# Block 0's last sums on VectorE, w_in's sums later on GpSimd, step 7's q and k ahead of a row of w_out

## The chip, the cores and the metric

The kernel runs on one core of a Trainium2 chip. The metric is the device time of one execution in microseconds; the kernel before took 661.88 us (median of three runs, 661.77 to 662.99). A core has five engines that run side by side, each with its own queue in which instructions start in order: TensorE (PE in the profile) multiplies matrices and writes to PSUM, VectorE (DVE) and ScalarE (ACT) do elementwise work, GpSimd (POOL) does elementwise work between SBUF tiles, and SyncE (SP) only starts transfers (DMAs). ACT and POOL start transfers too.

## The reference

Two stages. The first is a recurrent retention over 4 batches, 8 heads and 768 steps with heads of 64; its output, with the heads side by side, is the input x of 3072 tokens by 512. The second is a feed-forward layer with a quick GELU:

```
state = gamma * state + k_t v_t^T          (per batch and head)
y_t   = scale * q_t state
x     = y as 3072 x 512
h     = x @ w_in                           (512 x 2048)
out   = (h * sigmoid(1.702 h)) @ w_out     (2048 x 512)
```

All of it is computed in float32; the weights arrive as 64-bit floats.

## The kernel before

**Tiling.** The retention is done in chunks of 64 steps for two batches at once: 24 chunks, called steps j below. Four steps give the 512 tokens of one block; there are six blocks, m = 0 to 5. Each block goes through an up-projection (w_in, gate) and a down-projection (w_out). While block m is projected, the steps of the block after next are woven in (`step`, `turn`, `decay`), so that TensorE always has work.

**Fewer products.** Most projections are done by a scheme with seven products of half matrices in place of eight. It needs sums and differences of the inputs: of w_in (`sums_w1`, on GpSimd, four instructions for each of four pairs p of row groups), of w_out (`sums_w2`, and its t3 term `sums_w2_t3`, L542, on VectorE), of the gated hidden values g (`sums_g`, L546 to L548, VectorE; `sums_g_late`, L552, GpSimd) and of X (`sums_x`, L530 to L533, GpSimd). Block 0 computes its hidden values with plain products (`up0`) and keeps them where the sums of w_in will later lie: slots 4, 5 and 6 of the weights' tiles W1A and W1B hold its g in slots 0, 1 and 2; slot 3 lies in X and in a small tile g0 whose place is later that of kd. So sums_w1 can write slot 4 only after block 0's g slot 0 has been read for the last time, and so on.

**Stages in time.** 0 to 105 us: eight steps of the retention, the narrowing of the 64-bit weights to float32 (fetch on SP, `abs` on ScalarE, `half` and `rest` on VectorE) and block 0's up-projection, in an order written out by hand. 105 to 154: block 1's up-projection (`seven`). 154 to 204.5: block 0's down-projection. 204.5 to 261.5: block 1's. Then blocks 2 to 5, each some 100 us, with `up` (L562) and `down49` (L666), the last with a second level of seven products.

**Block 0's and 1's down-projection** (`down`, L799) is a list of 28 units, n = 0 to 27, of 1.73 us each: seven products of four units d. Product n // 4 = 2 reads slot 3 of g; after each of its units the three `sums_g` of that pair of rows are made, and the fourth product reads their result. Product 6 (units 24 to 27) reads slot 1 after `sums_g_late`. The third and fourth outputs are stored from GpSimd's queue after product 5 (`then_p7`, `put`), the last after product 6. Between the units the loop at the end of the kernel calls `sums_w2_t3` (block 0, units 8 to 11), `sums_w1` (block 1, units 3, 11, 19 and 27) and `inner_w2` (L612, differences of w_out, stored to W2D in DRAM from SP and GpSimd).

**Blocks 2 to 5** load those differences back: `stream` (L635) fetches for each i = 0 to 6 three pieces of 256 KB into half of a tile `ring`, with one DMA on GpSimd's queue. Piece 1 is read by the third pair of unit (i, 0), the fourth product in TensorE's order there, pieces 0 and 2 by unit (i, 1). The stream for i + 2 is called once the half is free, after unit (i, 1) and after `then`, which makes the output's additions (`put`, GpSimd, L692 to L695) and stores it (L696).

**What sets the order.** TensorE's queue is in the order of the code. On the other engines a scheduler places each instruction when, by its own estimate, its inputs are ready, so an instruction may run far ahead of its place in the code. `tc.keep_in_program_order(i)`, and `pin` as long as `ordered` is set, tie an instruction behind the one that the code issued before it on the same engine. In the first stage all is tied. `decay` (kd, L274) and `aged` (state, L359) of steps 9 and later are not.

**Loads.** Steps 6 and 7 load q and k in 8 DMAs each on SP (L157), then k again as kn and v (L143). `w9b w9a` in the written order are the two fetches (L180) of one row of w_out. From step 8 on, kn has a single buffer, which `decay` frees; `turn` transposes q and k on VectorE (L253) and then loads those two steps ahead.

Of the kernel before, what the change touches and what calls it, by code (L numbers as in the profile page):

```python
# [28 lines left out]
def kernel(  # L29
# [29 lines left out]
    pe, act, dve, pool, sp = nc.tensor, nc.scalar, nc.vector, nc.gpsimd, nc.sync  # L59
# [13 lines left out]
    NP = NFF // 2  # L73
# [19 lines left out]
    W2D = [dram.tile([P, 3, NP // 2, P], F32, name=f"W2D{i}") for i in range(7)]  # L93
    W2 = const.tile([P, 7, NP, EH], F32, name="W2")
# [426 lines left out]
    def sums_w1(p):  # L521
        t, q1 = w1(p)
        w = [t[:, q1:q1 + 2, s] for s in range(7)]
        pool.tensor_add(w[4], w[2], w[3])
        pool.tensor_sub(w[6], w[0], w[2])
        pool.tensor_sub(w[5], w[4], w[0])
        pool.tensor_sub(w[2], w[1], w[5])

    def sums_x():
        tc.keep_in_program_order(pool.tensor_sub(X[:, 4], X[:, 2], X[:, 0]))  # L530
# [8 lines left out]
        dve.tensor_sub(w[1], w[2], w[5])  # L539

    def sums_w2_t3(p):
        dve.tensor_sub(W2[:, 6, p:p + 2, :], W2[:, 5, p:p + 2, :], W2[:, 0, p:p + 2, :])  # L542

    def sums_g(m, p):
        a = [g(m, p, s) for s in range(4)]
# [3 lines left out]

    def sums_g_late(m, p):  # L550
        a = [g(m, p, s) for s in range(2)]
        tc.keep_in_program_order(pool.tensor_sub(a[1], a[1], a[0]))  # L552


    def up(d):
# [76 lines left out]
    def stream(ring, i):  # L632

        c = ring[:, i % 2 * 3:i % 2 * 3 + 3]
        pool.dma_start(c, W2D[i])  # L635
        return c

    def begin_ring():
# [4 lines left out]
    def down49(m, ring, comps):  # L643

        b, t0 = m * CB // NC * 2, m * CB % NC * D
# [37 lines left out]
        def put(th, e, half, y, a):  # L683
            if half == 0:
                kept[th, e] = two.tile([P, 7, P], F32, name="o")
            c = kept[th, e]
            dve.tensor_add(c[:, 4 * half:4 + 3 * half], y, kept[a][half])
            if half == 0:
                return
            last = m == NB - 1  # L690
            eng = dve if last else pool
            eng.tensor_add(c[:, 1:3], c[:, 1:3], c[:, 0:1].to_broadcast([P, 2, P]))  # L692
            eng.tensor_add(c[:, 3], c[:, 3], c[:, 2])
            eng.tensor_add(c[:, 0:5:4], c[:, 2:4], c[:, 4:5].to_broadcast([P, 2, P]))
            eng.tensor_add(c[:, 2:4], c[:, 0:4:3], c[:, 5:7])  # L695
            (act if last else pool).dma_start(rows[th, e], c[:, 1:5].rearrange("p (b f) e -> p b (f e)", b=2))  # L696

        def then(i, half, p0):
            if i == 0:
# [36 lines left out]
        for i in range(7):  # L736
            for half in range(2):
                def unit(i=i, half=half):
                    if half == 0:
                        if i == 0:  # L740
                            pairs[0] = derive(0)
                        x = "x" if i in (0, 2, 3) else "y"
                        if i != 2 and i != 3:
                            for n in range(2):
                                acc[x, n] = ps.tile([P, 4 - n, P], F32, name="pq", tag=x)
                    x = "x" if i in (0, 2, 3) else "y"
                    if i == 6 and half == 1 and m == NB - 1:
                        finish(acc[x, half], pairs[i][half])
                        return
                    products(acc[x, half], pairs[i][half], i not in (2, 3))  # L750
                    then(i, half, acc[x, half])
                    if half == 0 and i < 6:
                        pairs[i + 1] = derive(i + 1)
                    if half == 1:
                        if i + 2 < 7:
                            comps[i + 2] = stream(ring, i + 2)
                        if i in (0, 1, 3):
                            sums_g_outer((0, 1, None, 2)[i])
                todo.append(unit)
        return todo  # L760

    def down(m):

        acc, kept = {}, {}
        b, t0 = m * CB // NC * 2, m * CB % NC * D
# [58 lines left out]
        for n, d in order:  # L824
            key, sa, sb, new, last, then = P_[n]
            def unit(key=key, sa=sa, sb=sb, new=new, last=last, d=d, then=then, n=n):
                part(key, sa, sb, new, last, d, then)
                if n == 2:
                    sums_g(m, 2 * d)
                if n == 4 and d == 3:  # L830
                    for p in range(0, NP, 2):
                        sums_g_late(m, p)
            todo.append(unit)
# [110 lines left out]
    for name in """  # L944
        k0 table q0 warm turn0 w0b rows warm k1 abs0b q1 turned0 step0 v0 w0a half0b mask k2 turn1 causal rest0b
        masked0 decay0 v1 decay1 abs0a half0a step-0 updated0 turned1 q2 step1 rowd whole w2b turn2 w2a x0 k3
        aged1 masked1 turned2 v2 rest0a abs2 q3 step-1 updated1 state1 decay2 aged2 step2 q4 x1 half2 decay3 w3b
        w3a up0.0.0 masked2 turn3 k4 step-2 v3 q5 rest2 k5 gate0.0.0 turned3 updated2 state2 step3 up0.0.2
        masked3 abs3 half3 x2 rest3 turn4 w1b step-3 aged3 gate0.0.2 turned4 state3 w1a w5b updated3 v5 decay4
        abs1 x3 turn5 half1 up0.0.3 turned5 up0.1.2 step4 aged4 w5a rest1 v4 gate0.0.3 decay5 w6a masked4  # L950
        gate0.1.2 abs5 w6b step5-4 half5 rest5 up0.0.1 updated4 abs6 state4 gate0.0.1 w4b
        up0.1.1 half6 aged5 w4a up0.0.5 rest6 masked5 up0.1.5 gate0.1.1 x4 gate0.0.5 abs4 step-5 w8b w8a
        half4 gate0.1.5 state5 updated5 anew q6 up0.1.6 x5 rest4 gate0.1.6 abs8 v6 decay6 aged6 up0.0.6 w7b w7a half8
        turn6 gate0.0.6 up0.1.0 abs7 seven_4.2 seven_6.2 half7 gate0.1.0 w9b w9a up0.1.4 q7 gate0.1.4 step6 masked6 rest7 up0.0.4 v7
        gate0.0.4 seven_52.2 turn7 up0.1.3 gate0.1.3 step7-6 seven_4.0 masked7 updated6 decay7 aged7 abs9 state6 x6 up0.0.7 rest8 seven_w.0 gate0.0.7
        w11a w11b step-7 state7 x7 seven_x half9 w10b w10a up0.1.7 gate0.1.7
        seven2.0 seven2.1 abs11 rest9 seven2.2 seven_v.0 w12a w12b seven2.3 half11 seven2.4 abs10 seven_4.1 seven_w.1
        seven2.5 rest11 seven2.6 w14b w14a seven0.0 seven0.1 half10 seven0.2 abs12 seven0.3 rest10 w13a w13b seven0.4
        seven_v.1 seven0.5 seven_4.3 half12 seven_w.3 seven0.6 seven1.0 abs14 seven1.1 rest12 w15a w15b seven1.2 seven1.3
        half14 seven1.4 abs13 seven_v.3 seven1.5 updated7 rest14 seven1.6 seven3.0 seven3.1 half13 seven3.2 abs15 seven3.3  # L960
        rest13 seven3.4 seven3.5 late_loads half15 rest15 seven3.6 seven_end
    """.split():
        works[name]()
    ordered[0] = False
    INNER = [(0, 19), (0, 22), (0, 26), (1, 2), (1, 12), (1, 15), (1, 18)]
    for m in range(NB):
# [31 lines left out]
        for n, unit in enumerate(down(m) if m < 2 else down49(m, *ring)):  # L998
            unit()
            if m == 0 and n < NP and n % 2:  # L1000
                sums_w2(n - 1)
            if m == 0 and NP <= n < 3 * NP // 2:
                sums_w2_t3(2 * (n - NP))
            if m == 1 and n % 8 == 3:
                sums_w1(n // 4)
            if (m, n) in INNER:
                inner_w2(INNER.index((m, n)))
            if between and (n in (2, 5, 11, 16, 21) if m == 1 else n % 3 == (1 if m else 2)):
# [49 lines left out]
```

## Time and profile before

| what | value |
|---|---|
| median of three runs | 661.88 us |
| the profiled execution | 662.24 us |
| its span, from first to last instruction | 660.5 us |
| TensorE busy | 642.2 us (97%) |
| VectorE busy | 453.9 us (69%) |
| GpSimd busy | 198.8 us (30%) |
| ScalarE busy | 159.0 us (24%) |
| chain of waits: TensorE's share | 89% |
| GpSimd idle ahead of the ring's DMAs (L635) | 227.7 us |
| granted TensorE clock | 0.997 of full speed |

A row of the timeline gives the start, the length, the engine, the line of the kernel, the operation, the tile written and the tiles read, the shapes, the number of instructions merged, and in brackets the idle time of the engine just before with the instruction that ended it. A float32 matmul leaves two records. "SPq" is SP starting a DMA. The list of waits gives for each engine and line whom it waited for, in total, how often, and the longest. The chain of waits is followed back from the last instruction, each step to what released it.

### The profile page before, as it was taken

How to read it: one execution, taken by the hardware profiler on the slowest of the kernel's cores; microseconds unless marked ns; L12 is line 12 of the kernel's file. 1: busy time of each engine (PE TensorE's matmuls, PEld its weight loads, DVE VectorE, ACT ScalarE, POOL GpSimd, SP SyncE). 2: the span in 40 equal slices, each digit the busy share in tenths (PEclk: the TensorE clock that was granted, in tenths of full speed). 3: DMA queues.
4: the chain of work that ended last, by engine and by line, in shares of the span. 5: the costliest groups of instructions: out<-in, count | busy, mean ns of one | idle time of the engine just before them, and what ended most of it. 6: DMA issues, size and time to landing. Idle time of an engine off the chain costs nothing.

```text
span 660.5 us, 15291 instructions
## 1 busy us (share of the span) xinstructions
PE 642.2 (97%) x6390; PEld 580.2 (88%) x6390; DVE 453.9 (69%) x645; ACT 159.0 (24%) x306; POOL 198.8 (30%) x225
## 2 busy tenths in 40 slices
PE   6789999999999999999999999999999999999997
PEld 3778888888788888889999888999888999988997
DVE  3699989999936973556984445995354995254965
ACT  4674233551000000333100233010233110233110
POOL 6400311310379217000536400445600255500000
PEclk9989999999999999999999999999999999999999
DMA  9995549763233556262485832386742252602142
GB/s 176 193 274 173 152 104 241 172 163 60 49 82 135 137 149 153 58 248 96 118 199 134 279 57 97 86 223 135 225 118 97 66 154 104 235 21 96 55 154 96
DMA packets 148149, 91.86 MB, mean 139 GB/s; under 512 B 131600, under 2 KB 134416, under 8 KB 147056
## 3 DMA queue, kind: packets, MB, share of 16 engines
q1 hardware_dynamic: 135856, 45.19, 29.8%
q0 software_dynamic: 9888, 44.46, 20.6%
q10 hardware_dynamic: 2336, 1.25, 0.6%
q8 instruction: 50, 0.82, 0.5%
q14 instruction: 19, 0.16, 0.1%
HBM read 72.89 MB, written 15.47 MB: 134 GB/s over the span
## 4 chain that ended last, share of the span: by engine, by line
PE 89%; DVE 4%; DMA 4%; SPq 1%; issue 1%; ACT 0%; DVEq 0%
PE pq L666 27%; PE px L562 17%; PE pd L799 13%; PE py L562 13%; PE ph L491 7%; PE ph L414 5%; PE pa L289 2%; PE py L312 2%; PE pa L297 2%; PE py L306 2%; DMA W<-in_moe_w_in_dram 1%; DMA W<-in_moe_w_out_dram 1%; DMA q_in<-in_q_dram 1%; PE pt L250 1%; SPq L140 1%
## 5 line engine op out<-in xcount | busy, mean ns | idle before, releaser
L635 POOL DMA_DIRECT2D ring<-W2D x28 | 15.4, 551 | 227.7 <-PE px L562 118.3
L666 PE MATMUL pq<-W,G 128*128 128x128 f32 x672 | 80.2, 276 | 0.0
L666 PEld LDWEIGHTS pq<-W,G 128*128 128x128 f32 x672 | 77.6, 192 | 1.3 <-issue 0.7
L666 PE MATMUL pq<-ring,own 128*128 128x128 f32 x448 | 60.1, 276 | 1.3 <-issue 1.3
L562 PE MATMUL px<-X,W1A 128*128 128x256 f32 x256 | 59.8, 379 | 0.0
L562 PE MATMUL px<-X,W1B 128*128 128x256 f32 x256 | 59.8, 379 | 0.0
L666 PEld LDWEIGHTS pq<-ring,own 128*128 128x128 f32 x448 | 54.5, 192 | 0.4
L562 PEld LDWEIGHTS px<-X,W1B 128*128 128x128 f32 x256 | 48.5, 190 | 6.7
L562 PEld LDWEIGHTS px<-X,W1A 128*128 128x128 f32 x256 | 48.4, 190 | 6.5
L393 ACT ACTIVATE G<-G 128x512 f32<-128x512 f32 x60 | 37.4, 628 | 54.7 <-DVE G L572 33.4
L799 PE MATMUL pd<-W,G 128*128 128x256 f32 x224 | 49.6, 381 | 0.0
L799 PEld LDWEIGHTS pd<-W,G 128*128 128x128 f32 x224 | 42.2, 190 | 5.9
L562 PE MATMUL py<-X,W1A 128*128 128x256 f32 x192 | 45.4, 379 | 0.0
L562 PE MATMUL py<-X,W1B 128*128 128x256 f32 x192 | 45.4, 379 | 0.0
L562 PEld LDWEIGHTS py<-X,W1A 128*128 128x128 f32 x192 | 36.5, 190 | 5.0
L562 PEld LDWEIGHTS py<-X,W1B 128*128 128x128 f32 x192 | 36.5, 190 | 5.0
L580 DVE TENSOR_TENSOR t<-py,u 128x512 f32<-128x512 f32 x16 | 11.1, 692 | 32.3 <-PE py L562 32.3
L569 ACT ACTIVATE p<-px 128x512 f32<-128x512 f32 x16 | 9.6, 597 | 96.0 <-PE px L562 96.0
L414 PE MATMUL ph<-X,W1A 128*128 128x256 f32 x128 | 30.6, 397 | 0.9 <-DVE X L347 0.9
L594 DVE TENSOR_TENSOR G<-G 128x512 f32<-128x512 f32 (+2 forms) x24 | 12.3, 513 | 25.7 <-ACT G L393 25.7
L666 PE MATMUL pq<-ring,G 128*128 128x128 f32 x224 | 29.6, 275 | 0.0
L666 PE MATMUL pq<-W,own 128*128 128x128 f32 x224 | 29.6, 275 | 0.0
(237 smaller groups left out, 1226.0 us busy)
## 6 DMA issues: line engine op xcount, KB each, us to landing
ring<-W2D POOLq DMA_DIRECT2D x28, 768.0 KB, 4.8
W1B<-W1D POOLq DMA_DIRECT2D x6, 1792.0 KB, 9.8
W<-in_moe_w_in_dram SPq DMA_DIRECT2D x12, 512.0 KB, 5.9
W<-in_moe_w_out_dram SPq DMA_DIRECT2D x10, 512.0 KB, 5.8
out_dram<-o POOLq DMA_DIRECT2D x20, 256.0 KB, 3.0
q_sq<-in_q_dram SPq DMA_DIRECT2D x144, 32.0 KB, 2.1
k_sq<-in_k_dram SPq DMA_DIRECT2D x144, 32.0 KB, 2.1
v_in<-in_v_dram SPq DMA_DIRECT2D x72, 64.0 KB, 3.1
```

The lines of the kernel that those rows point to most:

```text
L289: pe.matmul(pa[HALF[w], u, 0, s, :], kt[HALF[u], w, s, :], qt[HALF[u], w, s, :], start=True, stop=True)
L297: pe.matmul(pa[HALF[u], w, 1, s, :], kd[HALF[w], HP * u + s, :], vn[HALF[w], HP * u + s, :], start=True, stop=True)
L306: pe.matmul(py[HALF[o], u, 1, 2 * w + s2, :], old[HALF[u], w, 2 * s2 + o, :], qt[HALF[u], w, 2 * s2 + o, :], start=True, stop=True)
L312: pe.matmul(py[HALF[o], w, 0, 2 * u + s2 if f < NEW else 2 * s2 + u, :], vn[HALF[w], HP * u + s, :], a[HALF[w], u, s, :], start=True, stop ...
L393: pin(act.activation(g, h[:, i], AF.Gelu_apprx_sigmoid))
L414: pe.matmul(h[:, ab], w, X[:, 2 * th + c // 2, c % 2, :], start=(ab == 0 and c == 0), stop=(c == 3), skip_group_check=True)
L491: pe.matmul(acc[:, u, :], w, x, start=(start and u == 0 and c == 0), stop=(stop and c == 1), skip_group_check=True)
L562: pe.matmul(acc[:, u, :], t[:, q1 + u, sa, c, :], X[:, sb, c, :], start=(start and u == 0 and c == 0), stop=(stop and c == 1), skip_group_ ...
L594: dve.tensor_sub(q[0][1], q[0][0], q[0][1])
L635: pool.dma_start(c, W2D[i])
L666: pe.matmul(p0[:, j, :], a[:, d], w[:, d], start=(new and j == 0 and d == 0), stop=(d == NP // 2 - 1), skip_group_check=True)
L799: pe.matmul(p0[:, n, :], g1(m, p, sa)[:, n * P:(n + 1) * P], W2[:, sb, p, :], start=(new and p == 0 and n == 0), stop=(last and p == NP - ...
```

## The change

Six edits:

- In block 0, the t3 sums of w_out are made after the last of the twelve g sums, in unit 11, and tied there; before, one was called after each of the units 8 to 11, untied.
- Block 0's four late g sums follow them, in the same unit and on VectorE; before, they were called after unit 19, on GpSimd. Block 1's stay where they were.
- The sums of w_in are called in block 0's units 24 to 27 and tied; before, they were called in block 1's units 3, 11, 19 and 27, untied.
- Step 7's q and k are loaded behind w7's two fetches and ahead of `half8` and w9's; before, behind w9's.
- Each stream of the ring is two tied DMAs, piece 1 first and then pieces 0 and 2, and is called ahead of `then`; before, one untied DMA after `then`.
- The output's store in `put` of `down49` (L696) is tied.

```diff
     def sums_w1(p):
...
-        pool.tensor_add(w[4], w[2], w[3])
-        pool.tensor_sub(w[6], w[0], w[2])
-        pool.tensor_sub(w[5], w[4], w[0])
-        pool.tensor_sub(w[2], w[1], w[5])
+        tc.keep_in_program_order(pool.tensor_add(w[4], w[2], w[3]))
+        tc.keep_in_program_order(pool.tensor_sub(w[6], w[0], w[2]))
+        tc.keep_in_program_order(pool.tensor_sub(w[5], w[4], w[0]))
+        tc.keep_in_program_order(pool.tensor_sub(w[2], w[1], w[5]))
...
     def sums_w2_t3(p):
-        dve.tensor_sub(W2[:, 6, p:p + 2, :], W2[:, 5, p:p + 2, :], W2[:, 0, p:p + 2, :])
+        tc.keep_in_program_order(dve.tensor_sub(W2[:, 6, p:p + 2, :], W2[:, 5, p:p + 2, :], W2[:, 0, p:p + 2, :]))
...
     def sums_g_late(m, p):
         a = [g(m, p, s) for s in range(2)]
-        tc.keep_in_program_order(pool.tensor_sub(a[1], a[1], a[0]))
+        tc.keep_in_program_order((pool if m else dve).tensor_sub(a[1], a[1], a[0]))
...
     def stream(ring, i):
 
         c = ring[:, i % 2 * 3:i % 2 * 3 + 3]
-        pool.dma_start(c, W2D[i])
+        for k in (slice(1, 2), slice(0, 3, 2)):
+            tc.keep_in_program_order(pool.dma_start(c[:, k], W2D[i][:, k]))
         return c
...
-            (act if last else pool).dma_start(rows[th, e], c[:, 1:5].rearrange("p (b f) e -> p b (f e)", b=2))
+            tc.keep_in_program_order((act if last else pool).dma_start(
+                rows[th, e], c[:, 1:5].rearrange("p (b f) e -> p b (f e)", b=2)))
...
                     products(acc[x, half], pairs[i][half], i not in (2, 3))
+                    if half == 1 and i + 2 < 7:
+                        comps[i + 2] = stream(ring, i + 2)
                     then(i, half, acc[x, half])
                     if half == 0 and i < 6:
                         pairs[i + 1] = derive(i + 1)
                     if half == 1:
-                        if i + 2 < 7:
-                            comps[i + 2] = stream(ring, i + 2)
                         if i in (0, 1, 3):
...
                 if n == 2:
                     sums_g(m, 2 * d)
-                if n == 4 and d == 3:
+                    if m == 0 and d == 3:
+                        for p in range(0, NP, 2):
+                            sums_w2_t3(p)
+                        for p in range(0, NP, 2):
+                            sums_g_late(m, p)
+                if m and n == 4 and d == 3:
                     for p in range(0, NP, 2):
                         sums_g_late(m, p)
...
-        half4 gate0.1.5 state5 updated5 anew q6 up0.1.6 x5 rest4 gate0.1.6 abs8 v6 decay6 aged6 up0.0.6 w7b w7a half8
-        turn6 gate0.0.6 up0.1.0 abs7 seven_4.2 seven_6.2 half7 gate0.1.0 w9b w9a up0.1.4 q7 gate0.1.4 step6 masked6 rest7 up0.0.4 v7
+        half4 gate0.1.5 state5 updated5 anew q6 up0.1.6 x5 rest4 gate0.1.6 abs8 v6 decay6 aged6 up0.0.6 w7b w7a q7 half8
+        turn6 gate0.0.6 up0.1.0 abs7 seven_4.2 seven_6.2 half7 gate0.1.0 w9b w9a up0.1.4 gate0.1.4 step6 masked6 rest7 up0.0.4 v7
...
-            if m == 0 and NP <= n < 3 * NP // 2:
-                sums_w2_t3(2 * (n - NP))
-            if m == 1 and n % 8 == 3:
-                sums_w1(n // 4)
+            if m == 0 and 3 * NP <= n < 7 * NP // 2:
+                sums_w1(2 * (n - 3 * NP))
```

## The prediction

> **What bounds the kernel now.** I read the page's busy times first, then TensorE's waits, then the timelines around each wait, and last the queues behind the code that moves.
>
> ```profile
> PE 642.2 (97%) x6390; PEld 580.2 (88%) x6390; DVE 453.9 (69%) x645; ACT 159.0 (24%) x306; POOL 198.8 (30%) x225
> ...
> PE 89%; DVE 4%; DMA 4%; SPq 1%; issue 1%; ACT 0%; DVEq 0%
> ```
>
> TensorE sets the end; the chain of waits is 89% matmuls. So only time that TensorE loses can be won back, and work taken off any other engine is worth nothing by itself. TensorE's waits, less those of the first 55 us, which no edit touches:
>
> ```profile
> PE pq L666 <- issue: 1.3, 2, 0.7
> PE pd L799 <- DVE W1B L548: 1.2, 2, 0.9
> ...
> PE pa L289 <- DVE G L253: 0.7, 1, 0.7
> ```
>
> Two of these lie beside the change: L548 is the last of block 0's sums of g, L253 the transposition of step 7's k. The timeline shows the first (start, length, engine; the bracket is idle time and who ended it):
>
> ```profile
> 174.10 1.58 POOL L552 TENSOR_TENSOR W1A<-W1A 128x512 f32<-128x512 f32 x1 [3.28 <-DVE W1A L548]
> ...
> 174.46 1.76 DVE L546 TENSOR_TENSOR X<-W1B,X 128x512 f32<-128x512 f32 x1
> ...
> 175.00 3.88 PE L799 MATMUL pd<-W,W1A 128*128 128x256 f32 x16
> ...
> 179.76 1.99 PE L799 MATMUL pd<-W,W1B 128*128 128x256 f32 x8 [0.89 <-DVE W1B L548]
> ...
> 180.23 0.68 DVE L318 TENSOR_TENSOR at<-pa,mask 128x512 f32<-128x512 f32 x1
> ...
> 182.04 1.99 PE L799 MATMUL pd<-W,W1B 128*128 128x256 f32 x8 [0.28 <-DVE W1B L548]
> 183.87 5.34 PE L799 MATMUL pd<-W,X 128*128 128x256 f32 x24
> ```
>
> The reader should take starts, not ends. 24 undisturbed records run from 167.37 to 172.55 (rows of the same view), so one takes 0.216 us. From 175.00 to 183.87 there are 32 records: 6.91 us of work in 8.87. TensorE loses **1.96 us** here, not the 1.2 that the waits admit. VectorE is late for two reasons in these rows: three of the four t3 sums (L542) stand ahead of the g sums, and GpSimd's L552 stretches two of VectorE's L546 from 0.68 to 1.76 us.
>
> The second wait, and the transfer on the chain behind it:
>
> ```profile
> 78.23 8.88 DMA W<-in_moe_w_out_dram
> ...
> 90.99 1.21 DMA k_sq<-in_k_dram
> ```
> ```profile
> 93.27 0.71 DVE L253 STREAM_TRANSPOSE G<-k_sq 128x512 f32<-128x512 f32 x1 [1.07 <-DMA k_sq<-in_k_dram]
> ...
> 94.13 0.69 PE L289 MATMUL pa<-G 64*64 64x64 f32 x32 [0.72 <-DVE G L253]
> ```
>
> SP's queue stood still until w9's two transfers had landed, issued the last q and all of k after that, and k came 1.07 us late. By starts, 16 records of L414 before this step take 4.35 us (89.78 to 94.13), and 16 before the next step 3.65 (96.15 to 99.80): **0.70 us** lost.
>
> **What the Trainium skill says.** "SBUF — State Buffer", section "Who interferes with whom": a VectorE instruction with two inputs in SBUF contends with a GpSimd instruction that reads SBUF, and the second to start blocks fully; with at most one SBUF input it doesn't. The trace agrees: L546 with two SBUF inputs went from 0.68 to 1.76 beside L552, while L318, with one input in PSUM, stayed at 0.68 beside the L552 of 179.85. "Perfetto Trace Analysis", section "Summary: the profiler window per engine type": a TensorE end is an estimate. The trace agrees: 16 records shown as 3.88 us are followed 4.76 after their start. "DMA: Bandwidth & Descriptors", section "Anatomy of one DMA — SWDGE (gpsimd) path", gives some 2.0 us plus bytes/436e3 for a GpSimd DMA: by that 3.8 us for 768 KB, where this trace has 4.8.
>
> **The change, part by part.**
>
> *Block 0's sums on VectorE.* The four t3 sums go behind all twelve g sums, and the four late sums (L552) leave GpSimd. With neither ahead, VectorE ends w_out's sums at 167.3, does two transpositions (1.25 us) and one output (0.6), and is at the g sums by 169.1, which is also when the matmuls that read the first pair's slot 3 end (167.37 + 8 x 0.216). Twelve sums at a pitch of 0.60 us, each pair held back by the matmuls that free it, end at about 170.9, 172.7, 174.5 and 176.4. TensorE wants them at 175.0, 176.7, 178.5 and 180.2, or 0.7 sooner once the other stall is gone. At least 3 us remain: -1.96. Four t3 (2.4 us) and four late sums (2.4) then run to about 181.9 with L318. Cover: VectorE was idle for 7.85 us before 191.04; t3 is first read at about 190.8, the late sums at 197.6. Without the cover it would cost up to 4.8.
>
> *w_in's sums.* GpSimd's sixteen instructions (rows of 1.27 to 1.72 us, 23.5 in all) ran between 181.4 and 213.3, eight of them before 199.3. They now follow the out stores of 199.56 to 201.05, with one more store (0.7) among them: 201.05 + 24.2 = 225 if nothing comes between. Their reader is block 2's first product, at 261.5: 36 us of room. What matters is GpSimd's queue around them: step 8's kd (191.02) waits for a freed slot and finds GpSimd idle, so it should stay ahead; step 9's kd (216.33) and state (219.72) now meet the sums, and VectorE's L612 and block 1's g sums (222.60 to 231.62) collide with the last ones. Bounds: below nothing, -0, since no TensorE wait of before lies here; above, see the rivals. I take 0: block 1's four pairs end at 224.73, 226.79, 228.85 and 231.62 and are read from 229.65 at 1.73 us intervals, so 3.3 us is the least room, and about three collisions of 1.08 fit.
>
> *Step 7's q, k ahead of w9.* Sixteen issues move past two on SP. They start at 77.7 instead of 78.7. The issues that waited for w9 can now wait for w7, which was there at 82.58 (ScalarE's L207 ended its wait then). Then eight k issues at 0.47: 86.3, plus 2.0 to landing (its row's median): 88.3, three us before VectorE reaches the transposition at 91.5. -0.70; between 0 and -0.7. w9 goes out at about 86.5 instead of 77.7 and lands, at 4.0 to 7.2 us, by 94; ScalarE reads it at 93.98. A microsecond more would be covered: the gate behind it came at 99.91 after 3.7 idle us, and VectorE asks for w9 only after 105. kn and v of step 7 stay behind w9, but SP reaches them no later than at 91.5.
>
> *Streams in two.* 28 more issues of 0.547 us on GpSimd, which stood idle 227.7 us before the present ones. By the skill's price a third is 2.6 us and two thirds 3.2, against 4.8 measured for the whole. Now ahead of the output's additions, the piece needed first goes out sooner: the one of 428.81 could go at 425.8, and its product starts at 436.93. TensorE never waited for the ring: 0. The kd at 418.68 loses at most 0.5 us and is used at 429.96.
>
> *Other pins* (stores, the sixteen sums): no instruction more, 0. The two "issue" waits of TensorE (1.3 us) have no releaser that the change touches: I leave them in, and they bound a further gain and loss.
>
> **Sum:** -1.96 - 0.70 = -2.66. Of the profiled execution (662.24, span 660.5) that makes a span of 657.8 and 659.6; the median of the runs is 0.36 below that execution, so **661.88 - 2.66 = 659.2 us**.
>
> **Rivals.**
>
> *Collisions in block 1.* Room 3.3 us; four late w_in sums cost 4 x 1.08 = 4.3, with two more on L612 6.5. TensorE then stalls 1.0 to 3.2 at about 235: 660.2 to 662.4, middle 661.0. For: GpSimd has 24 us of work from 201. Against: L612 gains in 191 to 199, where eight w_in sums are gone.
>
> *Nothing from q, k.* SP's order gains only the one microsecond of an earlier start and k still comes late: 661.88 - 1.96 = 659.9. Against: w9's 8.88 us on the chain.
>
> *Slower: GpSimd's queue.* If all sixteen sums stand ahead of step 9's kd, it starts at 225.3 instead of 216.33. The next k has one buffer, so its loads (218.94) wait for that kd: 7.8 us later. SP's rows follow each other without a gap from there to 265, so step 12's k is 7.8 late too; and block 2's sums of X stand behind its kd:
>
> ```profile
> 256.43 1.04 POOL L274 TENSOR_TENSOR kd<-kn_in,cold 128x512 f32<-128x512 f32 x1 [0.21 <-DMA kn_in<-in_k_dram]
> ...
> 261.53 1.27 POOL L532 TENSOR_TENSOR X<-X 128x512 f32<-128x512 f32 x1
> ```
>
> L532 would end at 270.6; the third product wants it at 264.97: 5.6 us lost, 661.88 - 2.66 + 5.6 = **664.8**. It decides once that kd is over 2.2 us late (264.97 - 262.80). Against: step 8's kd at 191.02 ran between sums of w_in, so GpSimd's order isn't the code's.
>
> **How the numbers follow.** A measurement tells about 0.2% from no change: 1.32 us, so faster is below 660.56 and slower above 663.20. Forecast 0.60, own range 658.2 to 660.2 (the issue waits going, or half a microsecond of collisions); collisions 0.17; nothing from q, k 0.08; GpSimd's queue 0.15. Faster: 0.60 + 0.08 = 0.68; same 0.17; slower 0.15. The range reaches over the forecast, the second rival and most of the collisions: 658.2 to 661.6.
>
> **What would show it.** Right: no TensorE wait on L548 at 173 to 184 and none on L253 near 94; starts 6.9 us apart over those 32 records; L546 always about 0.68 in block 0; k landed before 91; GpSimd's kd of step 9 within 2 us of its place. Wrong: a wait of L799 on block 1's L548 near 229 to 235 (first rival), or of px or py L562 on GpSimd's X sums near 262 (slower), or step 7 waiting for w9, v or kd in 94 to 100.

## The result, and the profile after

The changed kernel takes **663.75 us** (median of 20 runs, 660.82 to 665.91), the kernel before, beside it on the same chip, 661.95 (20 runs): ratio **1.0033, interval 1.0019 to 1.0047**. It is slower. 659.2 was predicted, with a range of 658.2 to 661.6. The profiled execution has a span of 660.8 us.

TensorE first. The chain's shares by engine on the page of the changed kernel:

```profile
PE 80%; DVE 7%; DMA 6%; SPq 4%; issue 1%; ACT 1%; DVEq 0%; ACTq 0%
```

The chain was 89% TensorE before and is 80% now; VectorE, DMAs and SP's queue have come onto it. The list of TensorE's waits says where (who waited for whom; total, times, longest):

```profile
PE pd L801 <- DVE G L548: 2.3, 2, 1.5
...
PE py L306 <- DVE X L347: 0.6, 1, 0.6
PE pa L289 <- DVE G L253: 0.4, 1, 0.4
```

L801 is the down-projection, L799 before. The wait on L548 is still there, but it is another one: it was at 180 us, in block 0, and is now in block 1. The table is worked out from the starts of TensorE's rows: each entry is the time from one landmark to the next, in the execution with a profile.

| stretch | before | after | difference |
|---|---|---|---|
| the 16 records ahead of step 7 | 4.35 | 3.97 | -0.38 |
| step 8 to the end of block 0's fourth product | 9.50 | 7.71 | -1.79 |
| from there to step 9 | 31.17 | 31.17 | 0 |
| step 9 to step 10 | 12.58 | 12.59 | 0 |
| step 10 to step 11 | 10.86 | 14.29 | **+3.43** |
| step 11 to step 12 | 10.85 | 11.14 | +0.29 |
| step 12 to block 2 | 12.03 | 12.91 | +0.88 |
| blocks 2 to 5 | 395.57 | 394.75 | -0.82 |

So block 0 gave what was forecast, and block 1's down-projection lost **4.60 us**. (The last row goes from block 2's first record to the end of TensorE's last. Ahead of 75 us, where the kernels of this study are the same, the start of one and the same step lies between 49.0 and 53.8 us in their profiled executions, so the spans are not compared.) The two places in TensorE's rows, block 0 and then block 1:

```profile
173.24 3.72 PE L801 MATMUL pd<-W,W1A 128*128 128x256 f32 x16
...
180.33 5.34 PE L801 MATMUL pd<-W,X 128*128 128x256 f32 x24
```
```profile
227.81 1.97 PE L801 MATMUL pd<-W,G 128*128 128x256 f32 x8 [1.49 <-DVE G L548]
230.62 7.83 PE L801 MATMUL pd<-W,G 128*128 128x256 f32 x32 [0.84 <-DVE G L548]
```

173.24 to 180.33 is 7.09 us for 32 records, where it was 8.87. In block 1 the fourth product waits twice for sums of g. Why those are late stands in VectorE's timeline around 215 us, first before the change, then after:

```profile
216.24 2.14 DVE L612 TENSOR_TENSOR X<-W,X 128x512 f32<-128x512 f32 x2
...
222.60 0.68 DVE L546 TENSOR_TENSOR G<-G 128x512 f32<-128x512 f32 x1
```
```profile
215.42 5.89 DVE L612 TENSOR_TENSOR X<-W,X 128x512 f32<-128x512 f32 x2
...
225.53 0.68 DVE L546 TENSOR_TENSOR G<-G 128x512 f32<-128x512 f32 x1
```

Step 9 starts at 215.0 before and at 211.5 after, so 222.60 is 7.6 us into it and 225.53 is 14.0: the sums of g begin 6.5 us later. Two L612 take 5.89 us in place of 2.14, which makes 3.75 of it, and all that is queued behind them on VectorE is pushed back. The other 2.7 us were there before these two began: they stand 3.9 us into step 9 and not 1.2. What GpSimd did during the two (changed kernel):

```profile
215.36 1.28 POOL L524 TENSOR_TENSOR W1B<-W1B 128x512 f32<-128x512 f32 x1
216.58 1.28 POOL L525 TENSOR_TENSOR W1B<-W1B 128x512 f32<-128x512 f32 x1
217.80 1.27 POOL L526 TENSOR_TENSOR W1B<-W1B 128x512 f32<-128x512 f32 x1
219.16 1.61 POOL L527 TENSOR_TENSOR W1B<-W1B 128x512 f32<-128x512 f32 x1
220.72 1.49 POOL L274 TENSOR_TENSOR kd<-kn_in,cold 128x512 f32<-128x512 f32 x1
```

These are the last four of the sixteen sums of w_in, and behind them step 9's kd. The first three follow each other at 1.22 us, each shown as starting before the one ahead has ended; only the fourth, which reads the third's result, leaves room. The chain of waits (start, length, who) takes the two L612 apart:

```profile
196.96 4.87 DVE X L612
...
215.42 4.23 DVE X L612
```

One L612, 0.68 us by itself, was held from 215.42 until 219.65: through **three** sums and not one. At 196.96 the same happened with 4.87 us, where the L612 in the same place took 2.42 before the change (at 200.49). The other 2.7 us come from there: each set of L612 waits until the store of the set ahead has landed, so the first hold is handed on. Counted from step 9, the set between the two begins 2.4 us later than before, and the one that meets the second hold 2.7. SP's queue of the changed kernel shows a second consequence: its store of the set that these L612 make stands ahead of the next loads.

```profile
221.34 0.32 SPq L613 DMA_DIRECT2D W2D<-X  x1
222.24 2.71 SPq L143 DMA_DIRECT2D kn_in<-in_k_dram  x4
```

That load starts 10.7 us into step 9; before, it was 3.9 (218.94). Whether that cost anything had to be tried.

### The profile page after: what moved, and what is told of

It is laid out like the page before. It is cut to its first block, busy times and chain, and to the rows that moved or that the text cites. A ratio compares the mean times of both kernels' runs of the same rounds, so it can differ in the third digit from the quotient of the medians.

```text
span 660.8 us, 15350 instructions
## 1 busy us (share of the span) xinstructions
PE 641.3 (97%) x6390; PEld 579.0 (88%) x6390; DVE 459.9 (70%) x649; ACT 159.3 (24%) x306; POOL 211.7 (32%) x249
## 4 chain that ended last, share of the span: by engine, by line
PE 80%; DVE 7%; DMA 6%; SPq 4%; issue 1%; ACT 1%; DVEq 0%; ACTq 0%
PE pq L667 27%; PE px L562 17%; PE py L562 13%; PE pd L801 8%; PE ph L491 7%; PE ph L414 4%; DMA W<-in_moe_w_in_dram 3%; DVE X L612 2%; SPq L157 2%; PE pa L289 1%; DMA G<-in_moe_w_in_dram 1%; SPq L143 1%; PE py L312 1%; PE py L306 1%; DMA W2D<-X 1%
## 5 line engine op out<-in xcount | busy, mean ns | idle before, releaser
L636 POOL DMA_DIRECT2D ring<-W2D x56 | 35.9, 643 | 221.6 <-PE px L562 117.8
L667 PE MATMUL pq<-W,G 128*128 128x128 f32 x672 | 80.2, 276 | 0.0
L667 PEld LDWEIGHTS pq<-W,G 128*128 128x128 f32 x672 | 77.6, 192 | 0.6
L667 PE MATMUL pq<-ring,own 128*128 128x128 f32 x448 | 60.0, 277 | 0.2 <-issue 0.2
L667 PEld LDWEIGHTS pq<-ring,own 128*128 128x128 f32 x448 | 54.6, 192 | 0.8 <-issue 0.4
L801 PE MATMUL pd<-W,G 128*128 128x256 f32 x224 | 50.4, 382 | 2.4 <-DVE G L548 2.3
L801 PEld LDWEIGHTS pd<-W,G 128*128 128x128 f32 x224 | 41.9, 190 | 9.5 <-DVE G L548 2.2
L580 DVE TENSOR_TENSOR t<-py,u 128x512 f32<-128x512 f32 x16 | 11.1, 691 | 32.0 <-PE py L562 32.0
L414 PE MATMUL ph<-X,W1A 128*128 128x256 f32 x128 | 29.0, 382 | 1.8 <-DVE X L347 1.1
L586 DVE TENSOR_TENSOR G<-py,vv 128x512 f32<-128x512 f32 x16 | 11.1, 692 | 26.6 <-ACT vv L583 26.6
L667 PE MATMUL pq<-W,own 128*128 128x128 f32 x224 | 29.6, 275 | 0.0
```

What stands on the lines that cost most here:

```text
L414: pe.matmul(h[:, ab], w, X[:, 2 * th + c // 2, c % 2, :], start=(ab == 0 and c == 0), stop=(c == 3), skip_group_check=True)
L580: dve.tensor_add(tt, z, u)
L586: dve.tensor_add(a[3], z, vv)
L636: tc.keep_in_program_order(pool.dma_start(c[:, k], W2D[i][:, k]))
L667: pe.matmul(p0[:, j, :], a[:, d], w[:, d], start=(new and j == 0 and d == 0), stop=(d == NP // 2 - 1), skip_group_check=True)
L801: pe.matmul(p0[:, n, :], g1(m, p, sa)[:, n * P:(n + 1) * P], W2[:, sb, p, :], start=(new and p == 0 and n == 0), stop=(last and p == NP - ...
```

## The experiments

The theory after these readings: VectorE's L612, which read twice from SBUF, are held by runs of GpSimd's sums, and all of the 4.60 us come from that, directly or handed on. The rival is the prediction's own third: the sixteen sums stand ahead of step 9's kd in GpSimd's queue, so kd and the loads behind it are late. Ratios are to the kernel before on the same chip.

| kernel | ratio | interval | g sums end | lost in block 1 |
|---|---|---|---|---|
| before | 1 | | 16.6 | 0 |
| the change | 1.0033 | 1.0019 to 1.0047 | 23.2 | 4.60 |
| e1, w_in's sums back | **0.9946** | 0.9929 to 0.9964 | 16.5 | 0.00 |
| e2, w_in's sums alone | 1.0102 | 1.0075 to 1.0129 | 24.6 | 6.15 |
| e3, block 0's sums alone | 0.9982 | 0.9970 to 0.9995 | 16.6 | 0.00 |
| e4, step 7's q, k alone | 0.9994 | 0.9983 to 1.0006 | 16.5 | 0.00 |
| e5, two fills per sum | 0.9950 | 0.9932 to 0.9968 | 16.5 | 0.00 |
| e6, another order of the sums | 1.0008 | 0.9992 to 1.0024 | 20.6 | 2.76 |
| e7, one L612 set later | 1.0142 | 1.0123 to 1.0161 | 18.3 | 12.47 |
| e8, streams and stores alone | 0.9983 | 0.9970 to 0.9997 | 16.6 | 0.00 |
| e9, three fills per sum | 0.9954 | 0.9936 to 0.9972 | 17.7 | 0.66 |
| e10, e3 and e4 together | 0.9983 | 0.9970 to 0.9995 | 16.6 | 0.00 |
| e11, fills, then kd | 0.9945 | 0.9930 to 0.9961 | 17.4 | 0.00 |
| e12, kd on ScalarE | 1.0031 | 1.0018 to 1.0045 | 23.9 | 5.16 |

The last two columns are in us. "g sums end" is the end of the last sum of g of block 1 on VectorE, counted from the start of step 9 on TensorE; "lost in block 1" is the time from step 9 to block 2 by TensorE's starts, less the 46.32 of before. But for e7 the two go together: nothing is lost up to 17.4, and beyond it some 0.8 us for each us of lateness (e9's 0.66 stands above that).

**The four parts.** e1 is the changed kernel with one part undone:

```diff
-        tc.keep_in_program_order(pool.tensor_add(w[4], w[2], w[3]))
+        pool.tensor_add(w[4], w[2], w[3])
...
-            if m == 0 and 3 * NP <= n < 7 * NP // 2:
-                sums_w1(2 * (n - 3 * NP))
+            if m == 1 and n % 8 == 3:
+                sums_w1(n // 4)
```

> The changed kernel with one edit undone: w_in's sums untied and called in block 1 again. Theory (the sixteen sums stand back to back on GpSimd from 197.5 to 220.7 and hold up VectorE's two-input L612, and with it step 9 and block 1's sums of g): the 4.2 us that TensorE lost between 226 and 251 go, and what block 0 and step 7 gained stays: some 2.5 us below the kernel before, a ratio of 0.996; L612 shows no instruction above 2.1 us, and L801 no wait on block 1's L548. Rival (the loss lies in the divided streams and ties of blocks 2 to 5, or in block 0): still about 1.003.

0.9946, and block 1 takes its old time to 0.01 us. Of the kernels here that compute the reference it is the fastest, faster than the two of the change. The set that was held in the changed kernel, in VectorE's timeline of e1:

```profile
214.07 2.13 DVE L612 TENSOR_TENSOR X<-W,X 128x512 f32<-128x512 f32 x2
```

It ends 3.3 us into step 9 (212.9), as before; in the changed kernel that was 9.8. Its sixteen sums were over by 211.2, 1.7 us ahead of step 9: eight of them had run by 197.1, the last four of these each as TensorE freed its slot. (e1 undoes the tie and the place of the calls together; the two weren't tried apart.)

e2 is the kernel before with that part alone, e3 with block 0's sums alone, e4 with `q7` moved alone, e8 with the streams and pinned stores alone (the hunks of the diff above, each by itself; of each the line that matters):

```diff
e2
-            if m == 1 and n % 8 == 3:
-                sums_w1(n // 4)
+            if m == 0 and 3 * NP <= n < 7 * NP // 2:
+                sums_w1(2 * (n - 3 * NP))
e3
-        tc.keep_in_program_order(pool.tensor_sub(a[1], a[1], a[0]))
+        tc.keep_in_program_order((pool if m else dve).tensor_sub(a[1], a[1], a[0]))
e4 (a piece of the line)
-        ... up0.0.6 w7b w7a half8
+        ... up0.0.6 w7b w7a q7 half8
e8
-        pool.dma_start(c, W2D[i])
+        for k in (slice(1, 2), slice(0, 3, 2)):
+            tc.keep_in_program_order(pool.dma_start(c[:, k], W2D[i][:, k]))
```

> The kernel before with that edit alone: w_in's sums tied and called in block 0's last units. Theory: block 1's loss comes with it whole, plus 4.2 us or 1.006, with one L612 above 4 us and TensorE waiting on block 1's L548. Rival (the loss needs the earlier arrival of block 0 that the other edits bring): below 2 us.

1.0102: more than expected, 6.15 us by stages. Most of the extra lies in step 9 (13.80 for 12.58). There the hold fell on the first L612 of the set, and the two behind it came later still:

```profile
216.84 4.71 DVE L612 TENSOR_TENSOR X<-W 128x512 f32<-128x512 f32 x1 [3.97 <-DMA W2D<-X]
```

So the size of the loss depends on which instruction meets the run of sums; the cause doesn't.

> The kernel before with block 0's t3 and late sums moved alone. The prediction's step says -1.96 us (0.997): no wait of L799's block 0 records on L548 and starts 6.9 us apart over the 32 records of its fourth product. Rival (VectorE takes back later what it gains, since it does four more sums): 1.000.

0.9982, that is -1.2 us (0.3 to 2.0), and 9.50 to 7.72 by stages.

> The kernel before with step 7's q and k loaded ahead of w9 alone. The prediction's step says -0.70 us (0.999): k is there before VectorE asks, and TensorE doesn't wait on L253. Rival from the changed kernel's trace: there TensorE still waited 0.36 us on L253 with k long landed, since VectorE itself was late; then about -0.35 us and no DMA wait on L253.

By time unclear (0.9994). By starts it is there: 3.55 us for the 16 records ahead of step 7 instead of 4.35, with no wait left, and the same 3.55 in e1 and e10. The changed kernel's profiled execution shows 3.97:

```profile
82.39 1.15 ACT L207 ACTIVATE W1B<-W 128x1024 f32<-128x1024 f32 x1 [4.09 <-DMA W<-in_moe_w_in_dram]
```

In that execution the weights' row ahead came late, and with it VectorE's queue, not k: TensorE waited 0.36 us for L253, and L253 waited for no transfer.

> The kernel before with the divided and tied streams and the tied stores alone. The prediction's step says 0 (1.000): blocks 2 to 5 take 101.4, 101.9, 100.1 and 92.3 us between the starts of their first products as before, apart from the two issue waits of up to 0.7 us. Rival (28 more issues on GpSimd delay its additions and kd): up to +1 us in those blocks.

0.9983: 1.1 us faster (0.2 to 2.0), where nothing was expected. Where it comes from stays open. Blocks 2 to 5 take 395.11 us on average in the nine executions that had this part and 395.62 in the five that had not, but the single ones run from 394.63 to 395.93 and from 395.16 to 396.19, so the means tell little. TensorE's waits for "issue" on L666 or L667 point the same way: 0.4 to 1.3 us in the five, 0 to 0.6 in the nine. Why the split or the order of the streams should shorten them isn't shown. e10 asked from the other side:

> The kernel before with two parts of the change only: block 0's sums on VectorE and step 7's q and k ahead of the row of w_out. Against the changed kernel with w_in's sums put back (0.9946) it lacks the split, earlier and tied streams and the tied stores. If these are worth nothing, as the prediction had it, 0.9946 to 0.995 here too; if they gained the 0.7 us by which blocks 2 to 5 were shorter on average in the executions that had them (394.96 against 395.69 us), about 0.996.

0.9983, against 0.9946 with the streams. That points to more than nothing for this part, and the profile shows at most half a microsecond of it. e10 itself leaves something open: by stages it gains 2.6 us, in block 0 and ahead of step 7, and by time 1.1 (0.3 to 2.0).

**Is it the reads?** e5 keeps the place of the sums but reads nothing: each is replaced by two fills.

```diff
-        tc.keep_in_program_order(pool.tensor_add(w[4], w[2], w[3]))
+        for _ in range(2):
+            tc.keep_in_program_order(pool.memset(w[4], 0.0))
...
```

> The changed kernel with each of w_in's sixteen sums replaced by two fills with zero of the same tile (blocks 2 to 5 then work on wrong weights): GpSimd is as busy in the same place and in the same order, step 9's kd still stands behind all of it, but it reads nothing from SBUF. Theory (the sums hold up VectorE because both read SBUF): L612 takes 0.7 us each, and TensorE's time from step 10 to step 11 returns from 14.3 to about 10.9 us; some 4 us below the changed kernel. Rival (it is GpSimd's queue, with kd, state and the loads behind it, that is late): the loss stays as far as the fills take as long as the sums.

0.9950, and no loss. GpSimd and VectorE of e5 (L616 is L612 here), beside each other:

```profile
205.13 1.11 POOL L527 MEMSET W1B<- 128x512 f32 x2
206.18 1.11 POOL L529 MEMSET W1B<- 128x512 f32 x2
```
```profile
206.17 1.42 DVE L616 TENSOR_TENSOR X<-W,X 128x512 f32<-128x512 f32 x2
```

Two L612 in 1.42 us, in the middle of unbroken fills: no hold. The Trainium skill says so too: "SBUF — State Buffer", section "Who interferes with whom", has the two-input VectorE instruction contend with a GpSimd instruction that reads SBUF, and not with one that only writes it. But GpSimd was done sooner as well (kd at 213.27, 3.6 us into step 9, against 9.2 in the changed kernel), so e5 alone doesn't exclude the rival.

> The changed kernel with each of w_in's sixteen sums replaced by three fills with zero that read nothing (48 in all), at the same place of GpSimd's queue; blocks 2 to 5 then work on wrong weights. By the 0.53 us of a fill in the run with two, GpSimd is busy for 25.2 us here, against 23.2 with the sums, so that step 9's kd comes later than in the changed kernel. Two terms are to be told apart, VectorE held by sums that read SBUF, and loads that come late behind that kd. Theory: the 3.4 us of step 10 come from the holding alone, so step 10 takes 10.86 again; the lateness costs only what the late q and k cost in steps 11 and 12, 1 to 3 us, since kd is 2.5 us later than in the changed kernel. In all 0.996 to 0.999 of the kernel before. Rival, all from the holding: 0.9945, as with two fills. Rival, GpSimd's queue alone (as the third rival of the prediction has it): 4.6 us or more lost, 1.003 or over.

It was meant to make kd as late without any reads, and failed at that. The scheduler put kd between the fills:

```profile
214.90 1.11 POOL L531 MEMSET W1B<- 128x512 f32 x2
215.98 1.03 POOL L274 TENSOR_TENSOR kd<-kn_in,cold 128x512 f32<-128x512 f32 x1
216.96 0.52 POOL L531 MEMSET W1B<- 128x512 f32 x1
```

So its 0.9954 says little about the rival. (One sum of g was stretched to 1.83 us beside the state, L359, which came late between the fills; 0.66 us was lost, all in step 12.) e11 ties kd behind the last of 44 fills, called ahead of it:

```diff
-        tc.keep_in_program_order(pool.tensor_add(w[4], w[2], w[3]))
...
+        for s in (4, 6, 5, 2):
+            for _ in range(3 if p else 2):
+                tc.keep_in_program_order(pool.memset(w[s], 0.0))
...
-            pin(pool.tensor_mul(KD[j]...
+            (tc.keep_in_program_order if j == 2 * CB + 1 else pin)(pool.tensor_mul(KD[j]...
...
-            if m == 0 and 3 * NP <= n < 7 * NP // 2:
-                sums_w1(2 * (n - 3 * NP))
+            if m == 1 and n == 5:
+                [sums_w1(p) for p in range(0, NP, 2)]
```

> As the run with three fills, but so that step 9's kd really comes late: 44 fills with zero in place of w_in's sixteen sums (two for each sum of the first pair of rows, three for the others; 23 us at 0.53, as long as the sums took), called in block 1's unit 5, and step 9's kd tied behind the last of them. In the run with three, the scheduler had put that kd between the fills. Blocks 2 to 5 again work on wrong weights. Here no GpSimd instruction reads SBUF while VectorE makes L612 and the g sums, but kd and the loads of k, v and q behind it are as late as in the changed kernel, 9 to 11 us after the start of step 9. Theory: step 10 takes 10.86 us as before the change; steps 11 and 12 lose 1 to 2 us together through late q and k; 0.996 to 0.998 of the kernel before. Rival, that kd's lateness makes the whole loss (the prediction's third rival): step 10 takes some 14.3 and the ratio is 1.002 or over.

0.9945, and no step of block 1 lost anything. GpSimd's and SP's rows show that kd and the load behind it were really late:

```profile
222.89 1.21 POOL L274 TENSOR_TENSOR kd<-kn_in,cold 128x512 f32<-128x512 f32 x1
```
```profile
224.12 2.63 SPq L143 DMA_DIRECT2D kn_in<-in_k_dram  x4
```

kd comes 9.3 us into step 9 (213.55), the load of k 10.6; in the changed kernel they came 9.2 and 10.7 us in. GpSimd was as busy up to there as with the sums, and no L612 took more than 0.69 us. **The rival falls**: a kd as late as that costs nothing by itself. The expectation of 1 to 2 us through late q and k in steps 11 and 12 falls with it. (Three of the four loads of v went ahead of k, so the q behind them started 14.0 us into step 9 and not 17.5 as in the changed kernel.) In the changed kernel too, VectorE's transpositions of q and k in block 1 stand without idle time ahead of them: they waited for no load.

e12 asks the reverse: the sums stay, and kd doesn't queue behind them.

```diff
+        elif j == 2 * CB + 1:
+            y, z = (a.rearrange("p (i s) d -> p i s d", i=2) for a in (KD[j], x))
+            for s in range(HP):
+                pin(act.activation(y[:, :, s], z[:, :, s], AF.Copy, scale=cold[:, H + s:H + s + 1]))
```

> The changed kernel with one instruction moved: step 9's kd is made on ScalarE (four activations with a scale by head) instead of on GpSimd behind the sixteen sums; everything computed stays. The sums still hold VectorE. Theory: step 10 loses 3.4 us as in the changed kernel. The loads gain little, because SP's store of the fourth set to W2D, ahead of them in its queue, waits for the held L612 until 221.3 anyway; so at most 0.5 us, 1.002 to 1.0035 of the kernel before. If instead the place of kd is what makes the loads late, steps 11 and 12 lose nothing and the ratio is 1.0015. Rival, that kd's lateness makes the whole loss: 0.995 to 0.996.

1.0031, as slow as the changed kernel, with 5.16 us lost: the hold is there and falls on the first L612 of the set, as in e2. kd is made at once on ScalarE, 1.3 us into step 9 (212.1), and still the load of k comes 11.1 us in, behind the same store, which waits for the held set. So e12 takes away the late kd, but not the late load. ScalarE, VectorE and SP of e12:

```profile
213.42 1.28 ACT L274 ACTIVATE kd<-kn_in,cold 128x128 f32<-128x128 f32 x4 [3.97 <-PE pa L298]
```
```profile
215.58 4.68 DVE L612 TENSOR_TENSOR X<-W 128x512 f32<-128x512 f32 x1 [4.00 <-DMA W2D<-X]
```
```profile
223.23 3.08 SPq L143 DMA_DIRECT2D kn_in<-in_k_dram  x4
```

**Is it the runs?** e6 makes the four sums depend on each other, one after the next.

```diff
         tc.keep_in_program_order(pool.tensor_add(w[4], w[2], w[3]))
-        tc.keep_in_program_order(pool.tensor_sub(w[6], w[0], w[2]))
         tc.keep_in_program_order(pool.tensor_sub(w[5], w[4], w[0]))
         tc.keep_in_program_order(pool.tensor_sub(w[2], w[1], w[5]))
+        tc.keep_in_program_order(pool.tensor_sub(w[6], w[0], w[2]))
```

Slot 6 is then made from the already overwritten slot 2, so blocks 2 to 5 work on other sums of w_in.

> The changed kernel with the four sums of each pair in the order w4, w5, w2, w6, where the second and third need the one before. In the changed kernel's trace L612 got in only after three sums that don't need each other, just ahead of one that does. Theory (a sum that must wait for its predecessor leaves VectorE a gap): the longest L612 falls from 4.9 to about 2 us and at least half of the 4.6 us lost in block 1 comes back, ratio to the kernel before about 0.998 to 1.000. Rival (each sum holds VectorE equally, whatever its order): still 1.003 and an L612 above 4 us.

1.0008, and the loss falls from 4.60 to 2.76 us. The set that took 5.89 us takes 3.32 (VectorE's timeline of e6):

```profile
212.52 3.32 DVE L612 TENSOR_TENSOR X<-W,X 128x512 f32<-128x512 f32 x2
```

VectorE begins block 1's sums of g 9.0 us into step 9, against 14.0 in the changed kernel and 7.6 before. That they end 4.0 us later than before has another reason: the dependent sums take 24.7 us on GpSimd instead of 23.2 (197.12 to kd's 221.83), and the last of them, kd and the state now meet the sums of g, three of which are stretched:

```profile
220.78 1.64 DVE L547 TENSOR_TENSOR G<-G 128x512 f32<-128x512 f32 x1
222.45 1.41 DVE L548 TENSOR_TENSOR G<-G 128x512 f32<-128x512 f32 x1
223.78 1.52 DVE L546 TENSOR_TENSOR G<-G 128x512 f32<-128x512 f32 x1
```

These are collisions of the kind that the prediction had priced, some 0.7 to 1.0 us each. So the short holds cost less than the long ones, and the same burst still costs 2.76 us.

**Can the held set be moved away?** e7 puts it nine units later.

```diff
-    INNER = [(0, 19), (0, 22), (0, 26), (1, 2), (1, 12), (1, 15), (1, 18)]
+    INNER = [(0, 19), (0, 22), (0, 26), (1, 11), (1, 12), (1, 15), (1, 18)]
```

> The changed kernel with the fourth set of differences of w_out (L612) called in block 1's unit 11 instead of 2, so that step 9's and block 1's sums of g no longer stand behind it on VectorE, while GpSimd keeps its order. Theory (TensorE waits because VectorE's queue stands behind a held L612): no wait on block 1's L548, step 10 to 11 back to about 10.9 us, with up to 2 us lost later where the differences now fall; ratio about 0.996 to 0.999. Rival (GpSimd's late kd and loads): the 3.4 us between steps 10 and 11 stay.

1.0142, a clear miss. SP's queue, VectorE's timeline and TensorE's waits in e7:

```profile
237.45 0.39 SPq L613 DMA_DIRECT2D W2D<-X  x1
```
```profile
243.25 0.69 DVE L612 TENSOR_TENSOR X<-W 128x512 f32<-128x512 f32 x1 [6.79 <-DMA W2D<-X]
```
```profile
PE pa L289 <- DVE kT L253: 7.2, 2, 6.0
```

The set's store now stands in SP's queue behind 24 loads. The next set needs the same part of X and waits for that store, and k's transposition is queued behind it on VectorE. The total therefore tells nothing of the sums; it shows what an instruction that waits cost here on an engine that works its queue off in order. One part of the expectation did hold: with no set in the way, block 1's sums of g begin 7.5 us into step 9, as before the change, and TensorE doesn't wait on L548, although the sixteen sums, kd (9.3 us into step 9) and the load behind it (10.8) are where the changed kernel has them.

## Why the prediction was wrong, point by point

**Block 0's sums, -1.96 us: right.** -1.79 by stages, 7.09 us for the 32 records where 6.91 was forecast. Every L546 of block 0 stayed at 0.69 or below, and the t3 and late sums ended at 183.3, with 4.25 idle us of VectorE behind them (181.9 and a larger gap were forecast). e3 confirms it alone.

**q and k, -0.70 us: right in kind.** -0.38 in the profiled execution, -0.80 in e1, e4 and e10. By time e4 alone can't tell it from none.

**Streams, 0: probably too low.** e8 measured -1.1 (0.2 to 2.0); not settled.

**w_in's sums, 0: the step that failed.** The prediction said "3.3 us is the least room, and about three collisions of 1.08 fit". The room was rightly read (3.2 by the rows); the price was not. 1.08 us was the stretch of an L546 beside a single L552. Here GpSimd had sums queued back to back, three in a row of which none reads the result of the one right before it, and one VectorE instruction was held through three of them: 3.55 us lost at 215.42 and 4.19 at 196.96. One such hold is more than the whole room. The prediction did have L612 among the instructions that meet the sums, but at 1.08 us apiece and with a gain to be expected from 191 to 199; and it didn't follow what stands behind L612. Both long holds fell on it. The first was handed on through the stores, the second stood seven instructions ahead of the g sums in VectorE's queue, and these came 6.5 us late. The +0.29 and +0.88 of steps 11 and 12 are, by VectorE's rows, the same lateness, not yet worked off: VectorE never stood idle from 215.42 until it waited for a store to W2D at 240.3.

That a hold can outlast one instruction could be read from the kernel before. In its blocks 2 to 5 one VectorE instruction with two SBUF inputs lies beside kd and state, which follow back to back and don't read each other's result:

```profile
535.55 2.26 DVE L655 TENSOR_TENSOR own<-G 128x512 f32<-128x512 f32 x1
```
```profile
535.21 1.05 POOL L274 TENSOR_TENSOR kd<-kn_in,cold 128x512 f32<-128x512 f32 x1
536.21 1.05 POOL L359 TENSOR_TENSOR state<-state,whole_h 128x512 f32<-128x512 f32 x1
```

It ends 0.55 us after the second of them.

**The queue order: half right.** Of GpSimd the prediction said that "GpSimd's order isn't the code's" and that kd would stay near its place. It did not: with the sums tied, all sixteen stood ahead of step 9's kd, as the third rival had it. But that rival's price, 5.6 us through late sums of X, was wrong. TensorE itself was 4.6 us late, L532 at 264.11 kept nobody waiting, a late kd cost nothing in e11, and an early one gained nothing in e12. That the time came out near that rival's 664.8 is luck. The first rival, collisions in block 1, had the place and the kind (the wait of the fourth product on L548 near 229, which the prediction named as its mark, is there), and with 661.0 was too small by the same mis-sized term.

**The sum** with measured terms: -1.79 - 0.38 + 4.60 - 0.82 = +1.6 us, beside +2.2 (1.3 to 3.1) by the ratio. Without the failed step it would be -3.0 and, with a step 7 as in e1, -3.4; e1 measured -3.6 (2.4 to 4.7). The -0.82 of blocks 2 to 5 is no larger than the spread of that stretch between single executions, so it is in part luck that the sums come this near.

**Two readings of lines.** The prediction took "16 records shown as 3.88 us are followed 4.76 after their start" as a sign that TensorE's ends are estimates; its own row shows a wait of 0.89 us in that place. Its other row serves better: 24 records shown as 5.34 us from 167.37 are followed at 172.55, 5.18 after their start. And SP's queue didn't stand still until w9's transfers had landed: seven of the eight q were issued by 85.1. The last of them and k were late all the same, and moving them past w9 did away with the wait (e4).

**The gain that was there** is in e1: leave w_in's sums untied in block 1, where the scheduler runs eight of them ahead of 197.1 and the rest before step 9's kd can start. Then the other parts of the change show.

## What to carry to other kernels

Price the worst case of a collision between VectorE and GpSimd by the longest run of GpSimd instructions that can follow there without waiting for one another, not by one of them; a burst that is harmless by its sum can hold one VectorE instruction longer than the whole slack behind it. Before elementwise work is gathered in one place and tied, read which two-input VectorE instructions lie beside it and what is queued behind those, DMA issues on other queues included. When two causes fit (a held engine, a late load), build the pair that has one without the other, and look whether it really does: e11 had the late kd and the late load without the holding and lost nothing; e12 had the holding with kd on time and lost all, but its load was still late, since the held L612 itself makes it so.

## What the runs showed of the hardware that was not expected

- A VectorE instruction with two SBUF inputs can be held through several GpSimd instructions that follow back to back. L612 (0.68 us alone) took 4.23 and 4.87 us in the changed kernel and 4.7 to 4.8 in five more places of e2, e7 and e12. In all seven it got its turn where the first GpSimd sum stands that reads the result of the one before it (L527, behind L524 to L526). With every sum dependent on the one ahead (e6), two L612 took 3.32 us in place of 5.89. Whether the gap at such a dependence is what lets VectorE in, or something that goes with it, wasn't tried apart.
- Not every row of independent sums holds for long. In the changed kernel two L612 that followed each other took 1.64 us each, and the second, from 209.32, got its turn between L524 and L525, of which neither reads the other's result:

```profile
207.64 3.32 DVE L612 TENSOR_TENSOR X<-W,X 128x512 f32<-128x512 f32 x2
```
```profile
208.70 1.72 POOL L524 TENSOR_TENSOR W1B<-W1B 128x512 f32<-128x512 f32 x1
210.37 1.72 POOL L525 TENSOR_TENSOR W1B<-W1B 128x512 f32<-128x512 f32 x1
```

  There L524 had itself been stretched. In the seven long holds GpSimd came from starting a store and L524 took its usual 1.27 to 1.28 us. Which difference decides isn't shown.
- The one that starts first isn't safe. In six of the seven long holds L612 had, by the profile's starts, begun 0.4 to 0.6 us ahead of L524 and was held all the same (at 215.42 it began 0.06 us after). The rule that the prediction took from the Trainium skill ("SBUF — State Buffer", section "Who interferes with whom"), that the second to start blocks, doesn't account for these; the measurement decides.
- GpSimd pays too: sums that don't wait for the one before follow at 1.22 us, and those beside which VectorE got its turn took 1.60 to 1.72.
- A fill of 128x512 on GpSimd takes 0.53 us and does not hold L612 at all, 32 or 44 of them in a row (e5, e11).
